# Seven block products for eight in the gate and value products of three FFN units (sparse attention and gated FFN, one core)

## The chip, the cores and the metric

The kernel runs on one core of one Trainium2 chip. The metric is the device time of one execution in microseconds. The core's engines are TensorE (PE), VectorE (DVE), ScalarE (ACT), GpSimd (POOL) and SyncE (SP, which only issues DMAs here). Each engine works through its own queue in order; semaphores tie them together. The program is written with a fixed order: nothing decides at run time which step comes next.

## The reference, cut to what matters

```
# 1. attention: q, k, v are [4, 8, 768, 64]; chunks of 32 keys, each query may use its 6 best chunks
ub     = sum(max(q * k_min(chunk), q * k_max(chunk)))      # bound of a chunk, causal
scores = q @ k.T / 8, masked to the 6 chunks with the largest ub and to earlier keys
attn   = softmax(scores) @ v
# 2. FFN: x is [3072, 512], the 8 heads side by side
gate = 1 / (1 + exp(-(x @ w_gate)))        # w_gate [512, 1536]
val  = x @ w_val                           # w_val  [512, 1536]
out  = (gate * val) @ w_out                # w_out  [1536, 512]
```

## The kernel before, in words

The 24 blocks of 128 queries (four batches of six) are worked in eight units, u0 to u7; units 1 to 7 have up to three blocks, 384 tokens. For each unit the kernel prepares keys and queries, chooses chunks, runs attention (`attend`, L880: scores on TensorE, exponentials on ScalarE, causal mask on GpSimd, attention times values on TensorE) and leaves the transposed result `xT` in SBUF, four tiles of 128 input features by 384 tokens in f16. Then `ffn` (L1062) makes the FFN of the unit.

In `ffn` the 1536 hidden features are 12 column blocks (`fb`) of 128. For each, TensorE makes the gate product `g` (four matmuls of 384 columns, L1078) and the value product `v` (four more) into a PSUM bank each. ScalarE takes tanh of half the gate (L1087), and VectorE makes `hg = (tanh + 1) * v` from SBUF and PSUM (L1091); the missing factor 0.5 is applied at the output. `hg` is f16.

The output product has two forms. Units 0 to 3 use plain matmuls (L1119) and a copy out of PSUM (L1128). Units 4 to 7 use `pair` (L989): two token blocks of 128, two halves of every group of four hidden blocks and two halves of the output columns make a 2 x 2 by 2 x 2 block product, which is computed with seven block products (p1 to p7, L1013) for eight, in Winograd's form. It needs sums of blocks beforehand (`sw` and `sx`, L1000, on VectorE or GpSimd; of the output weights `tw`, L984, made once) and additions afterwards (L1030, VectorE, from PSUM). The third token blocks of two neighbouring units are held (`held`, L409 and L411 by engine) and paired with each other (u45, u67).

The order of everything is written out: the string `ORDER` (L96) names each step with its engine in the order in which it is emitted, and `SLOTS` (L250) fixes which slot of a rotating buffer each tile takes (PSUM has eight slots, `ps`, of a bank each). `plan.add` names a step with the engines that it may use and its dependencies; `Plan.order` (L77) reads the two strings. The costs that stand beside the steps do not reach the program.

Of the kernel before, what the change touches and what calls it, by code (L numbers as in the profile page):

```python
# [8 lines left out]
F32 = mybir.dt.float32  # L9
# [99 lines left out]
hq0=V mx0_u1=V ap0_u1=V apt0_u1=V hqm0_u1_0=G v_u0_0=P v_u0_2=P v_u0_3=P hg_u0_3=V wo0=G hkp111=G ubn1_u1=V tanh_u0_0=A hq0_u1_1=A
tanh_u0_1=A hg_u0_0=V v_u0_1=P hg_u0_1=V hg_u0_2=V v_u0_7=P v_u0_4=P hqm0_u1_2=A sc_u1_0_2=P exp_u1_0_2=A sc_u1_2_2=P sc_u1_2_0=P  # L110
sc_u1_0_1=P sc_u1_2_1=P exp_u1_0_1=A v_u0_5=P g_u0_5=P tanh_u0_5=A hq1_u1_0=V kcr1=V hk0_u1_3=V hg_u0_5=V g_u0_7=P tanh_u0_7=A
wo1=G hk0_u1_1=G hq1_u1_2=G hkf1=G hk1_u1_0=G hq1_u1_3=G exp_u1_2_1=A g_u0_4=P tanh_u0_4=A hg_u0_7=V ubm1_u1=V mx1_u1=V ap1_u1=V
apt1_u1=V sc_u1_3_2=P exp_u1_3_2=A exp_u1_2_2=A exp_u1_2_0=A cm_u1_2=G sc_u1_1_0=P sc_u1_1_2=P sc_u1_3_1=P exp_u1_1_2=A v_u0_6=P
sc_u1_0_0=P sc_u1_3_0=P g_u0_6=P exp_u1_3_1=A exp_u1_1_0=A tanh_u0_6=A exp_u1_3_0=A hg_u0_4=V hg_u0_6=V sc_u1_1_1=P v_u0_9=P
v_u0_8=P v_u0_10=P g_u0_10=P tanh_u0_10=A exp_u1_1_1=A hg_u0_10=V g_u0_9=P tanh_u0_9=A g_u0_11=P tanh_u0_11=A exp_u1_0_0=A
g_u0_8=P tanh_u0_8=A v_0_3=S wo2=G cm_u1_3=G hqm1_u1_2=G v_0_1=S v16_0_1=G v_0_2=S v16_0_3=G v16_0_2=G pv_u1_3=P pv_u1_2=P
hqm1_u1_0=G sc_u1_4_2=P exp_u1_4_2=A sc_u1_4_1=P sc_u1_5_1=P exp_u1_5_1=A exp_u1_4_1=A sc_u1_5_2=P o0_u0_0=P rz_u1_1=V x_u1_1=V
hg_u0_9=V xps_u1_1=P xT_u1_1=V exp_u1_5_2=A sc_u1_4_0=P exp_u1_4_0=A cm_u1_0=G pv_u1_0=P cm_u1_1=G pv_u1_1=P rz_u1_0=V hg_u0_8=V
x_u1_0=V sc_u1_6_0=P exp_u1_6_0=A sc_u1_6_2=P exp_u1_6_2=A sc_u1_7_0=P v_u0_11=P sc_u1_6_1=P q2_u2=S k0_u2=S kn_u2_0=A qn_u2_2=G
qT_u2_2=P exp_u1_6_1=A sc_u1_7_2=P exp_u1_7_2=A qf_u2_2=V hq0_u2_2=A sc_u1_7_1=P xps_u1_0=P sc_u1_5_0=P xT_u1_0=A exp_u1_5_0=A  # L120
exp_u1_7_1=A kT_u2_0=P kx1_u2_0=V o0_u0_1=P exp_u1_7_0=A qf1_3=S cm_u1_6=G pv_u1_6=P o1_u0_0=P hg_u0_11=V kt_u2_0=V o2_u0_0=P
kx0_u2_0=V q0_u2=S k2_u2=S kn_u2_2=A kT_u2_2=P kx0_u2_2=V kx1_u2_2=V kt_u2_2=V cm_u1_5=G qn_u2_0=G qT_u2_0=P cm_u1_7=G pv_u1_7=P
rz_u1_3=V osb_u0_0=A pv_u1_5=P q3_u2=S qn_u2_3=G cm_u1_4=G qT_u2_3=P k1_u2=S kn_u2_1=A kT_u2_1=P kx0_u2_1=V pv_u1_4=P k3_u2=S
kn_u2_3=G kT_u2_3=P hk0_u2_0=G hq1_u2_2=G qf_u2_0=A hq1_u2_0=G q1_u2=S qn_u2_1=A qT_u2_1=P o1_u0_1=P kf1_3=S kf0_3=S kfT_3=P
kt_u2_1=A qf_u2_1=A hk1_u2_1=A rz_u1_2=V x_u1_3=V x_u1_2=V xps_u1_2=P xps_u1_3=P qf0_3=S qfT_3=P o2_u0_1=P kx1_u2_3=V kx0_u2_3=V
vf1_3=G qm_u2_1=G qm_u2_0=G hk1_u2_0=A qm_u2_2=A qf_u2_3=A qm_u2_3=A xT_u1_3=V kx1_u2_1=V kcr_u2=G ub_u2=P xT_u1_2=A hk0_u2_2=A
kf16_3=V qf16_3=A scf_3=P vf_3=S vc_3=A out_u0_0=S expf_3_1=A expf_3_0=A hq0_u2_3=A hk0_u2_1=G hq0_u2_0=G kt_u2_3=A g_u1_0=P
g_u1_1=P tanh_u1_0=A o0_u0_2=P osb_u0_1=V hq0_u2_1=V hq1_u2_1=A tanh_u1_1=A cmf_3_0=G pvf_3_0=P o1_u0_2=P o2_u0_2=P osb_u0_2=A
ubn0_u2=V ubn1_u2=V mx1_u2=V mx0_u2=V ap1_u2=V rzf_3_0=V apt1_u2=V cmf_3_1=G hqm1_u2_0=G sc_u2_5_2=P xf_3_0=V pvf_3_1=P
sc_u2_4_0=P exp_u2_4_0=A xpsf_3_0=P sc_u2_4_1=P exp_u2_5_2=A exp_u2_4_1=A sc_u2_5_1=P sc_u2_5_0=P exp_u2_5_0=A ap0_u2=V apt0_u2=V  # L130
hqm0_u2_0=V sc_u2_0_1=P exp_u2_0_1=A sc_u2_0_0=P xTf_3_0=V rzf_3_1=V sc_u2_1_0=P sc_u2_1_2=P xf_3_1=V v_u1_0=P hg_u1_0=V
sc_u2_0_2=P g_u1_2=P v_0_4=S hqm1_u2_2=G hqm0_u2_2=G v_0_5=S v16_0_5=G hq1_u2_3=G v16_0_4=G exp_u2_0_0=A cm_u2_0=G cm_u2_5=G
# [226 lines left out]
def kernel(  # L359
# [17 lines left out]
    T = 384  # L377
# [684 lines left out]
    def ffn(u, base, span):  # L1062
# [4 lines left out]
        for fb in range(NFB):  # L1067
# [17 lines left out]
            if fb % 2 == 0:  # L1085
                plan.hold(op, hg)
# [171 lines left out]
```

## Time and profile before

| What | Value |
|---|---|
| Runs of the kernel before | 289.1, 288.9 and 289.47 us, median 289.1 |
| The profiled execution's own time | 288.62 us |
| Its span, first to last instruction | 286.6 us |
| Output product of unit 4 begins | 199.84 us |
| Last TensorE instruction ends | 282.8 us |

The profile shows one execution. A busy time is the time in which at least one instruction of that engine was under way. A group of instructions has its line, engine, operation and tiles (`out<-in`), the count, the busy time, the mean length of one in ns, and the idle time of its engine just before them with what ended it. A row of the timeline has start, length, engine and line, and the number of merged instructions (`x3`). A row of waits has the engine that waited, the one that released it, the total in us, the number of waits and the longest. Line numbers are those of the kernel before.

### The profile page before, as it was taken

How to read it: one execution, taken by the hardware profiler on the slowest of the kernel's cores; microseconds unless marked ns; L12 is line 12 of the kernel's file. 1: busy time of each engine (PE TensorE's matmuls, PEld its weight loads, DVE VectorE, ACT ScalarE, POOL GpSimd, SP SyncE). 2: the span in 40 equal slices, each digit the busy share in tenths (PEclk: the TensorE clock that was granted, in tenths of full speed). 3: DMA queues.
4: the chain of work that ended last, by engine and by line, in shares of the span. 5: the costliest groups of instructions: out<-in, count | busy, mean ns of one | idle time of the engine just before them, and what ended most of it. 6: DMA issues, size and time to landing. Idle time of an engine off the chain costs nothing.

```text
span 286.6 us, 7277 instructions
## 1 busy us (share of the span) xinstructions
PE 272.8 (95%) x2764; PEld 186.3 (65%) x2764; DVE 212.3 (74%) x615; ACT 186.9 (65%) x392; POOL 148.2 (52%) x233
## 2 busy tenths in 40 slices
PE   3878999999999999999999999999999999999994
PEld 2654566667755765556677548767876786676673
DVE  3678846687999989796989997866725756373785
ACT  5688578779976965369999769997763402514210
POOL 6567773768394803926677765655611080130430
PEclk9999999999999999999999999999999999999999
DMA  7999999999999994799950030000020020000124
GB/s 166 238 221 195 196 204 223 249 174 204 175 206 188 163 193 104 160 162 243 173 113 2 0 113 2 2 0 2 2 77 0 1 75 0 2 0 0 68 81 183
DMA packets 123377, 32.69 MB, mean 114 GB/s; under 512 B 111440, under 2 KB 120400, under 8 KB 123344
## 3 DMA queue, kind: packets, MB, share of 16 engines
q1 hardware_dynamic: 118592, 27.53, 45.9%
q0 software_dynamic: 4752, 4.72, 9.8%
q8 instruction: 21, 0.34, 0.5%
q14 instruction: 12, 0.10, 0.1%
HBM read 30.67 MB, written 6.29 MB: 129 GB/s over the span
## 4 chain that ended last, share of the span: by engine, by line
PE 81%; DMA 12%; SPq 2%; POOL 1%; DVE 1%; issue 1%; DVEq 0%
PE g_u L1078 19%; PE v_u L1078 19%; PE sc_u L896 11%; PE o_u L1119 10%; PE p_u L1013 9%; PE pv_u L929 6%; DMA wo<-in_moe_w_out_dram 5%; DMA wg<-in_moe_w_gate_dram 4%; PE ube_u L835 2%; DMA kq_u<-in_q_dram 2%; PE xps_u L956 1%; SPq L586 1%; DMA kf<-in_k_dram 1%; SPq L575 1%; DVE ox L1030 1%
## 5 line engine op out<-in xcount | busy, mean ns | idle before, releaser
L907 ACT ACTIVATE att_u<-sc_u 128x512 f16<-128x512 f32 (+3 forms) x184 | 86.8, 570 | 5.0 <-PE sc_u L896 2.5
L1087 ACT ACTIVATE gate_u<-g_u 128x384 f16<-128x384 f32 x96 | 47.1, 503 | 58.4 <-PE g_u L1078 53.1
L1091 DVE SCALAR_TENSOR_TENSOR hg_u<-gate_u,v_u 128x384 f16<-128x384 f16 x96 | 50.8, 543 | 36.0 <-PE v_u L1078 20.9
L1078 PE MATMUL g_u<-xT_u,wg 128*128 128x384 f16 x384 | 73.2, 326 | 0.9 <-DMA wg<-in_moe_w_gate_dram 0.9
L1078 PE MATMUL v_u<-xT_u,wv 128*128 128x384 f16 x384 | 72.5, 326 | 0.0
L1078 PEld LDWEIGHTS <-wg 128*128 128x128 f16 x384 | 36.0, 98 | 24.5 <-DMA wg<-in_moe_w_gate_dram 1.8
L1078 PEld LDWEIGHTS <-wv 128*128 128x128 f16 x384 | 36.2, 98 | 22.9 <-issue 0.5
L913 POOL TENSOR_SCALAR_AFFINE_SELECT att_u<-att_u 128x384 f16<-128x384 f16 (+1 forms) x56 | 28.2, 514 | 36.1 <-ACT att_u L907 30.6
L1119 PE MATMUL o_u<-wo,hg_u 128*128 128x512 f16 x144 | 34.6, 379 | 0.4 <-DMA wo<-in_moe_w_out_dram 0.3
L929 PE MATMUL pv_u<-v,att_u 128*128 128x65 f16 x640 | 26.6, 193 | 0.0
L929 PEld LDWEIGHTS <-att_u 128*128 128x128 f16 x640 | 24.5, 98 | 2.2
L896 PE MATMUL sc_u<-hqo,hko 128*128 128x128 f16 (+2 forms) x220 | 25.7, 243 | 0.0
L896 PE MATMUL sc_u<-hqe,hke 128*128 128x128 f16 (+2 forms) x220 | 25.1, 243 | 0.0
L1119 PEld LDWEIGHTS <-hg_u 128*128 128x128 f16 x144 | 13.5, 98 | 13.9 <-issue 0.6
L612 POOL CAST v<-v 128x512 f16<-128x512 f32 x23 | 13.7, 613 | 15.0 <-DMA v<-in_v_dram 14.7
L896 PEld LDWEIGHTS <-hke 128*128 128x128 f16 x220 | 16.7, 98 | 5.3 <-ACT xT_u L407 0.6
L896 PEld LDWEIGHTS <-hko 128*128 128x128 f16 x220 | 16.2, 98 | 4.3 <-DVE hqo L409 0.2
L636 POOL TENSOR_SCALAR qm_u<-qf_u 128x768 f32<-128x768 f32 (+3 forms) x10 | 16.2, 1617 | 3.3 <-PE ubo_u L835 2.0
L1030 DVE SCALAR_TENSOR_TENSOR sw<-p_u,sw 128x256 f32<-128x256 f32 (+1 forms) x20 | 10.6, 529 | 6.1 <-PE p_u L1013 5.7
L948 DVE TENSOR_TENSOR x_u<-pv_u,rz_u 128x384 f16<-128x384 f32 (+1 forms) x28 | 14.5, 525 | 0.4
L858 DVE MAX8 mx_u<-ubn_u 128x8 f32<-128x8 f32 (+16 forms) x152 | 12.6, 159 | 0.3
L1128 ACT ACTIVATE osb_u<-o_u 128x512 f32<-128x512 f32 x10 | 6.0, 596 | 10.1 <-PE o_u L1119 10.1
(159 smaller groups left out, 442.5 us busy)
## 6 DMA issues: line engine op xcount, KB each, us to landing
v<-in_v_dram SPq DMA_DIRECT2D x23, 256.0 KB, 4.4
k<-in_k_dram SPq DMA_DIRECT2D x12, 384.0 KB, 5.5
q<-in_q_dram SPq DMA_DIRECT2D x12, 384.0 KB, 5.5
out_dram<-osb_u SPq DMA_DIRECT2D x12, 256.0 KB, 3.4
out_dram<-sw SPq DMA_DIRECT2D x8, 256.0 KB, 2.0
wg<-in_moe_w_gate_dram POOLq DMA_DIRECT2D x3, 512.0 KB, 11.5
wv<-in_moe_w_val_dram POOLq DMA_DIRECT2D x3, 512.0 KB, 11.2
wo<-in_moe_w_out_dram POOLq DMA_DIRECT2D x3, 512.0 KB, 13.2
```

The lines of the kernel that those rows point to most:

```text
L612: plan.add(f"v16_{b}_{ib}", {POOL: pool(H * D)}, lambda e: nc.gpsimd.tensor_copy(v16[b % 2][:, ib, :, 0:D], at(t)), reads=[t], writes=[("v ...
L636: (nc.vector if e == DVE else nc.gpsimd).tensor_scalar_max(o, i, 0.0)
L896: nc.tensor.matmul(at(t)[:, o:o + 128 * m], hk[b % 2][e_][:, p, 128 * jb:128 * jb + 128], hq[u.side][e_][:, p, 128 * x:128 * (x + m)], sta ...
L907: plan.add(f"exp_{u.name}_{h}_{y}", {ACT: act(n)}, lambda e, t=t, att=att, b0=b0, n=n: nc.scalar.activation(at(att)[:, b0:b0 + n], at(t), ...
L913: nc.gpsimd.affine_select(out=dv, in_=dv, compare_op=ALU.is_ge, fill=0.0, base=0, pattern=[[0, u.m], [1, 128]], channel_multiplier=-1)
L929: nc.tensor.matmul(at(pv)[:, last, x, :], at(att)[:, c:c + 128], v16[b % 2][:, jb, h, :], start=(jb == 0), stop=(jb == ib))
L948: plan.add(f"x_{u.name}_{p}", {DVE: dve(u.t)}, lambda e: nc.vector.tensor_tensor(at(x_).rearrange("p a (e d) -> p e a d", e=2), at(pv)[:, ...
L1013: nc.tensor.matmul(at(to)[:, side], a(j)[:, i], b(j)[:, i], start=j == i == 0, stop=j == 2 and i == 1)
L1078: nc.tensor.matmul(at(t), w16[:, c, 128 * fb:128 * fb + 128], at(u.xt)[:, c, :], start=(c == 0), stop=(c == 3))
L1087: plan.add(f"tanh_{u.name}_{fb}", {ACT: act(T)}, lambda e, g=g, gate=gate: nc.scalar.activation(at(gate), at(g), AF.Tanh, scale=0.5), read ...
L1091: plan.add(f"hg_{u.name}_{fb}", {DVE: dve(T)}, lambda e, w_=w_, gate=gate, hg=hg, fb=fb: nc.vector.scalar_tensor_tensor(at(hg)[:, fb % 2], ...
L1119: nc.tensor.matmul(at(o), at(hgs[fc // 2])[:, fc % 2, 128 * tb:128 * tb + 128], wo16[:, fc, lo:hi], start=(fc == 0), stop=(fc == NFB - 1))
```

## The change

In units 5, 6 and 7 part of the gate and value products also goes by seven block products. Two neighbouring column blocks of 128 hidden features, two halves of the 512 input features and two halves of 192 tokens make the 2 x 2 by 2 x 2 product. `BY7` says which: column pairs 1 to 4 (blocks 2 to 9) of units 5 and 6, pairs 1 and 2 (blocks 2 to 5) of unit 7, gate and value each; 20 products of pairs. The other column blocks keep the plain products.

- For a pair there are seven products of two matmuls of 192 columns (`by7`), in four PSUM banks (p1; p2 and p6; p5 and p3; p7 and p4), where there were eight matmuls of 384 columns in two banks.
- The weights' sums (`ss`, four f16 sums of 256 elements for each of the eight weight pairs, 32 in all) are made once, those of x (`tt`, four f16 sums of 384 for each unit, 12 in all) for each unit.
- After the products, a copy `m1` takes p1 out of PSUM, and six additions per pair make the four blocks in f32 in SBUF (`c11` of 384 elements; `c4`, `c3`, `c12`, `c22`, `c21` of 192). For value pairs all six are on VectorE and read PSUM. For gate pairs (`SLOW7`) three copies on ScalarE (`m26`, `m53`, `m74`, 384 elements each) first bring the products into SBUF as f32, and the additions are spread over VectorE (25) and GpSimd (35).
- tanh and `hg` of these column blocks read the f32 result from SBUF and not from PSUM.
- Space: the copies lie in the first key buffer (`hk[0]`), free once unit 6's scores are made; the weights' sums in the buffers of raw v and in `v16[0]`; the sums of x in `hk[0]` or in the unit's query buffer.
- `ffn(units[5])` is planned behind the attention of unit 6 and no longer ahead of it. `ORDER` and `SLOTS` are new throughout the kernel: 1826 steps became 2140 (40 removed, 354 added: TensorE 140, VectorE 124, ScalarE 48 and GpSimd 42 of the added), and 162 of the steps that both have changed their engine.

```
+    SLOW7 = {(u, "g", i) for u in (5, 6, 7) for i in (1, 2, 3, 4)}
+    BY7 = {u: {(m, i) for i in (1, 2, 3, 4)[:2 if u == 7 else 4] for m in "gv"} for u in (5, 6, 7)}
...
+    def sums_of(u, next_):
...
+                w, out_ = blocks_of(m, i), ss[m, i]
+                for n, (a, b, op) in enumerate(((lambda w=w: w(1, 0), lambda w=w: w(1, 1), ALU.add), (out_[0][1], lambda w=w: w(0, 0), ALU.subtract),
+                                                (lambda w=w: w(0, 0), lambda w=w: w(1, 0), ALU.subtract), (lambda w=w: w(0, 1), out_[1][1], ALU.subtract))):
+                    plan.add(f"ss{n}_{m}{i}", {DVE: dve(256, 2), POOL: pool2(256)}, lambda e, a=a, b=b, op=op, o=out_[n][1]: both(e).tensor_tensor(
+                        o(), a(), b(), op), ...
...
+        for n, (a, b) in enumerate(((lambda: x_(0, 1), lambda: x_(0, 0)), (lambda: x_(1, 1), lambda: t_(0)),
+                                    (lambda: x_(1, 1), lambda: x_(0, 1)), (lambda: x_(1, 0), lambda: t_(1)))):
+            plan.add(f"tt{n}_{u.name}", {DVE: dve(384, 2), POOL: pool2(384)}, lambda e, a=a, b=b, n=n: both(e).tensor_tensor(
+                t_(n), a(), b(), ALU.subtract), ...
...
+    def by7(u, m, i, next_, views):
...
+        def product(p, to, side, a, b, reads):
+            def emit(e):
+                for c in range(2):
+                    nc.tensor.matmul(at(to)[:, side], a()[:, c], b()[:, c], start=c == 0, stop=c == 1)
...
+        p1, p26, p53, p74 = bank("p1", 1), bank("p26"), bank("p53"), bank("p74")
+        op = product("p1", p1, 0, lambda: w(0, 0), lambda: x_(0, 0), [])
+        product("p2", p26, 0, lambda: w(0, 1), lambda: x_(1, 0), [])
+        product("p6", p26, 1, s7[1][1], lambda: t_(1), tk(1))
+        product("p5", p53, 0, s7[0][1], lambda: t_(0), tk(0))
+        product("p3", p53, 1, s7[3][1], lambda: x_(1, 1), [s7[3][0]])
+        product("p7", p74, 0, s7[2][1], lambda: t_(2), tk(2))
+        product("p4", p74, 1, lambda: w(1, 1), lambda: t_(3), [(f"tt{u.i}", 3)])
...
+        move("m1", p1, lambda: v_(2), 1, [p1], [q[2]])
+        if slow:
+            tmp = Buf("tm", f"tm_{name}", [128, 3, 2, 192])
+            move("m26", p26, lambda: at(tmp)[:, 0], 2, [p26, ("tt5", 0)], [(tmp, 0)])
+            move("m53", p53, lambda: at(tmp)[:, 1], 2, [p53], [(tmp, 1)])
+            move("m74", p74, lambda: at(tmp)[:, 2], 2, [p74], [(tmp, 2)])
...
+        def onto(p, n, src, dst, other, reads, writes):
+            plan.add(f"{p}_{name}", {POOL: pool2(192 * n), DVE: dve(192 * n)} if slow else {DVE: dve(192 * n)}, lambda e: both(e).tensor_tensor(
+                dst(), src[0](), other(), ALU.add), ...
+        onto("c11", 2, a26, lambda: v_(0, 2), lambda: v_(2).to_broadcast([128, 2, 192]), [q[2]], [q[0], q[1]])
+        onto("c4", 1, a5, lambda: v_(3), lambda: v_(1), [q[1]], [q[3]])
+        onto("c3", 1, a7, lambda: v_(2), lambda: v_(1), [q[1]], [q[2]])
+        onto("c12", 1, a3, lambda: v_(1), lambda: v_(3), [q[3]], [q[1]])
+        onto("c22", 1, a7, lambda: v_(3), lambda: v_(3), [q[3]], [q[3]])
+        onto("c21", 1, a4, lambda: v_(2), lambda: v_(2), [q[2]], [q[2]])
...
     def ffn(u, base, span):
...
+                if seven[0]:
+                    gs = by7(u, "g", fb // 2, next_, views)
+                if seven[1]:
+                    vs = by7(u, "v", fb // 2, next_, views)
...
-    ffn(units[5], 6.0, 0.95)
...
     attend(units[6], 6.0)
+    ffn(units[5], 6.0, 0.95)
```

More of the change, by code (lines that the diff above doesn't have):

```diff
@@ L331 @@
+p7_u67:5 p4_u67:1
 """
@@ L397, in at @@
     def at(b):
+        if b.tile is None and b.kind == "tm":
+            b.tile = hk[0][b.slot].rearrange("p a s -> p (a s)")[:, 0:2304].bitcast(F32).rearrange("p (n x r) -> p n x r", n=3, x=2)
         if b.tile is None:
@@ L1060, in store @@
             dma=((hi - lo) * 1.35, 2048 if hi - lo > 256 else 512))
+    SLOW7 = {(u, "g", i) for u in (5, 6, 7) for i in (1, 2, 3, 4)}
+    BY7 = {u: {(m, i) for i in (1, 2, 3, 4)[:2 if u == 7 else 4] for m in "gv"} for u in (5, 6, 7)}
+    combos = sorted(set().union(*BY7.values()), key=lambda w: (w[1], "vg".index(w[0])))
+    old = [("v16", 0, ib) for ib in range(NBLK)]
+    keys0 = [("hk", 0, jb, e_, p) for jb in range(NBLK) for e_ in range(2) for p in range(NP)]
+    ss = {}
+    for n, w in enumerate(combos):
+        if n < 6:
+            b = Buf("v", f"ss_{w[0]}{w[1]}", [128, 4, 2, 128], F16)
+            ss[w] = [((b, x), lambda b=b, x=x: at(b)[:, x]) for x in range(4)]
+        else:
+            ss[w] = [(("ss", n, x), lambda n=n, x=x: v16[0].rearrange("p a h d -> p (a h d)")[
+                :, 1024 * (n - 6) + 256 * x:1024 * (n - 6) + 256 * x + 256].rearrange("p (i f) -> p i f", i=2)) for x in range(4)]
@@ L1067, in ffn @@
         for fb in range(NFB):
-            g = ps(f"g_{u.name}_{fb}", "ff", [128, T])
-            w_ = ps(f"v_{u.name}_{fb}", "ff", [128, T])
-            gate = Buf("gate", f"gate_{u.name}_{fb}", [128, T], F16)
+            seven = [u.i in BY7 and (m, fb // 2) in BY7[u.i] for m in "gv"]
             if fb % 2 == 0:
                 hgs.append(Buf("hg", f"hg_{u.name}_{fb // 2}", [128, 2, T], F16))
+                if seven[0]:
+                    gs = by7(u, "g", fb // 2, next_, views)
+                if seven[1]:
+                    vs = by7(u, "v", fb // 2, next_, views)
             hg = hgs[-1]
+            gate = Buf("gate", f"gate_{u.name}_{fb}", [128, T], F16)
             def product(t, w16, fb=fb):
```

573 lines of the change are left out of this document (331 added, 242 removed), and 2 rows, old and new, of the table plan.

## The prediction

> **What bounds the kernel now.** I read the page first, then TensorE's waits, then the windows.
>
> ```profile
> span 286.6 us, 7277 instructions
> PE 272.8 (95%) x2764; PEld 186.3 (65%) x2764; DVE 212.3 (74%) x615; ACT 186.9 (65%) x392; POOL 148.2 (52%) x233
> PE   3878999999999999999999999999999999999994
> PEclk9999999999999999999999999999999999999999
> PE 81%; DMA 12%; SPq 2%; POOL 1%; DVE 1%; issue 1%; DVEq 0%
> ```
>
> TensorE (PE) is busy for 95% of the span at full clock, and it is 81% of the chain that ended last. So a product less is worth its full length, as long as TensorE still gets its operands and its PSUM banks in time. Next, the windows: from 40 us to the first output product of unit 4, from there to TensorE's last product, the tail, and one earlier stretch for comparison.
>
> ```profile
> 40.00:199.84 159.84, 159.40 (x1817) 106.67 (x1816) 132.71 (x403) 128.85 (x275) 97.87 (x149) 1.00 0.69 132
> 199.84:282.80 82.96, 82.26 (x711) 59.44 (x709) 50.60 (x126) 29.98 (x66) 23.57 (x38) 1.00 0.10 36
> 282.80:286.60 3.80, 0.01 (x1) 0.00 (x0) 0.82 (x2) 0.00 (x0) 0.00 (x0) 1.00 0.39 138
> 80.00:100.00 20.00, 20.00 (x193) 12.00 (x192) 19.16 (x56) 16.27 (x37) 14.83 (x22) 1.00 1.00 185
> ```
>
> The columns are PE, PE's weight loads, DVE, ACT and POOL. All of the seven-product work lies in the second row. There TensorE idles 0.70 us in 82.96, VectorE (DVE) is busy 50.60, ScalarE (ACT) 29.98 and GpSimd (POOL) 23.57. TensorE's only wait there is this one:
>
> ```profile
> PE p_u L1013 <- DVE held L409: 0.7, 1, 0.7
> ```
>
> So that stretch has free time on three engines and none on TensorE. The question is whether 82.96 us has room for what the change puts on those three.
>
> **What it removes: 2.84 us of TensorE.** Three pieces of the chain in order of time (start, length, instructions) and one group:
>
> ```profile
> 206.49 0.91 PE pv_u L929 x30
> 217.56 1.95 PE v_u L1078 x12
> 230.84 6.11 PE p_u L1013 x56
> L929 PEld LDWEIGHTS <-att_u 128*128 128x128 f16 x640 | 24.5, 98 | 2.2
> ```
>
> One matmul costs 0.91/30 = 30.3 ns at 65 columns, 6.11/56 = 109.1 ns at 256 and 1.95/12 = 162.5 ns at 384. The line between the first two gives 82.7 ns at 192. A pair of column blocks takes 8 x 162.5 = 1300 ns now and 14 x 82.7 = 1158 ns then: 142 ns less, 20 times, is 2.84 us. A weight load lasts 98 ns, more than 82.7, but the 65-column matmuls come every 30.3 ns with one load each, so loads overlap and I charge nothing. Without that overlap a pair takes 14 x 98 = 1372 ns, 72 more than now.
>
> The Trainium skill's "TensorE: Matmul & The Clock Gate", section "Back-to-back issue gap", speaks against the change: it gives a sustained 81 ns per matmul at 128 columns and 131 at 512. On its line 192 columns would cost 89 ns and 384 columns 114 ns, so a pair would grow from 915 to 1251 ns, an estimate of 6.7 us lost in all. The rows (30.3 at 65, 162.5 at 384) lie on neither of its figures, so the trace decides and the sum doesn't use it.
>
> **What it adds to VectorE: about 30 us in the same stretch.** The lengths come from these rows:
>
> ```profile
> 226.85 0.55 DVE L948 TENSOR_TENSOR x_u<-pv_u,rz_u 128x384 f16<-128x384 f32 x1
> 227.31 0.18 DVE L946 RECIPROCAL rz_u<-pv_u 128x6 f32<-128x6 f32 x1
> 228.51 0.28 DVE L1000 TENSOR_TENSOR sw<-hg_u,hg_u 128x256 f16<-128x256 f16 x1
> 228.72 0.28 DVE L1000 TENSOR_TENSOR sx<-held,hg_u 128x256 f16<-128x256 f16 x1
> L1030 DVE SCALAR_TENSOR_TENSOR sw<-p_u,sw 128x512 f32<-128x512 f32 x8 | 5.5, 688 | 3.2 <-PE p_u L1013 3.1
> L1030 DVE SCALAR_TENSOR_TENSOR sw<-p_u,sw 128x256 f32<-128x256 f32 x12 | 5.1, 423 | 2.9 <-PE p_u L1013 2.5
> ```
>
> Back to back, the next instruction starts 0.09 us before the last one ends: 0.46 us from start to start at 384 elements, 0.21 for an f16 sum of 256. An addition from PSUM grows by (688 - 423)/256 = 1.04 ns an element, so 192 elements last 0.36 us and cost 0.27. The order that the new kernel fixes puts these on VectorE after unit 4's first output product (in both kernels TensorE has about 190 us of work, by these spacings, queued ahead of it):
> - value pairs, all on VectorE: 10 x (one of 384, five of 192) = 10 x 1.81 = 18.1 us;
> - gate pairs, VectorE's part: 4 of 384 and 21 of 192 = 7.5 us, and 2 moves, 0.5;
> - 15 of the 32 weight sums at 0.21 and 11 of the 12 sums of x at 0.27: 6.2 us. The other weight sums stand earlier, beside full TensorE work; I charge nothing for them.
>
> That is 32.3 us. Against it, 8 sums, 4 copies and 2 scalings move to the other engines, and a few steps of unit 7's attention move in: about -2.3. VectorE goes from 50.60 to 80.6 us where TensorE needs 82.96 - 2.84 = 80.1. The 50.60 counts instructions that stood alone at full length; if all but a third of those 126 overlap by 0.08 us, it falls by 6 to 7, to 74. I take the middle, 77.
>
> **What it adds to the others.**
>
> ```profile
> L984 POOL TENSOR_TENSOR tw<-wo,tw 128x512 f16<-128x512 f16 x2 | 2.3, 1152 | 0.0
> L1000 POOL TENSOR_TENSOR sw<-sw,hg_u 128x256 f16<-128x256 f16 x4 | 2.7, 670 | 9.7 <-DVE sw L1000 9.6
> L1087 ACT ACTIVATE gate_u<-g_u 128x384 f16<-128x384 f32 x36 | 16.9, 491 | 41.4 <-PE g_u L1078 38.4 <-DVE hg_u L1091 3.0
> ```
>
> GpSimd grows by (1152 - 670)/256 = 1.88 ns an element: 0.55 us at 192 and 0.91 at 384. Six of 384 and 29 of 192 are 21.4 us; with 3 weight sums, one sum of x, 7 more sums for the output and 2 copies, some 30 us: 23.6 becomes 53. ScalarE gets 30 moves of 384 (0.49 each) and 18 shorter ones, about 20 us: 50 of 80. Neither is the bound by itself.
>
> **What VectorE and GpSimd do to each other.** No row has f32 sums on both engines at once. The nearest:
>
> ```profile
> 202.10 2.29 POOL L1000 TENSOR_TENSOR sw<-hg_u,sw 128x256 f16<-128x256 f16 x3 [0.83 <-DVE sw L1000]
> 202.21 0.84 DVE L984 TENSOR_TENSOR tw<-wo,tw 128x512 f16<-128x512 f16 x1
> 208.29 0.42 DVE L984 TENSOR_TENSOR tw<-wo,tw 128x512 f16<-128x512 f16 x1
> 121.27 2.29 POOL L612 CAST v<-v 128x512 f16<-128x512 f32 x4
> 122.94 0.92 DVE L863 TENSOR_TENSOR ap<-ubn_u,mx_u 128x288 f16<-128x288 f32 x1
> 126.62 0.46 DVE L863 TENSOR_TENSOR ap<-ubn_u,mx_u 128x288 f16<-128x288 f32 x1
> L984 DVE TENSOR_TENSOR tw<-wo,tw 128x512 f16<-128x512 f16 x4 | 2.0, 522 | 0.0
> L1000 DVE TENSOR_TENSOR sx<-hg_u,hg_u 128x256 f16<-128x256 f16 x4 | 1.6, 409 | 0.0
> L1000 DVE TENSOR_TENSOR sx<-sx,held 128x256 f16<-128x256 f16 x3 | 1.2, 403 | 1.0 <-POOL sx L1000 1.0
> ```
>
> A VectorE sum with both inputs in SBUF takes twice its time when GpSimd is in an instruction: 0.84 for 0.42, 0.92 for 0.46, in f16 and from f32. The means show what that costs over the stretch: the last three groups lose (522 - 420) x 4, (409 - 280) x 4 and (403 - 280) x 3 ns, 1.3 us over 11 instructions. The other 28 output sums there run close to 0.28, so I spread 1.3 to 2.2 us over some 39: up to 0.056 each, while GpSimd was busy 28% of the time. In the new kernel GpSimd is busy 53 of 80 us, 66%, and about 105 VectorE instructions have both inputs in SBUF: 30 output sums, 15 weight sums, 11 sums of x, 4 of the output weights, 25 gate additions, and 20 gate-times-value steps whose value now lies in SBUF and not in PSUM (that last kind is not shown by any row). The upper end is 105 x 0.056 x 66/28 = 14 us; the lower end is nothing, if the order keeps them apart. I take 5, nearer the lower end, because most of today's sums meet nothing.
>
> The Trainium skill says in "SBUF — State Buffer", section "Who interferes with whom", that a VectorE instruction with two SBUF inputs and a GpSimd instruction that reads SBUF exclude each other for their whole length. The pairs 0.84/0.42 and 0.92/0.46 agree; what it makes of the sum is a rival below.
>
> **The sum.** VectorE: 77 + 5 = 82 us. It can't be fed without a gap: in the densest earlier window it was busy 19.16 of 20, so 82 takes 82 x 20/19.16 = 85.6 us, against 82.96 now: +2.6. Each value pair holds four of the eight PSUM banks until VectorE's last addition, and TensorE's queue is in order, so a late addition stops the next pair's first product and the plain products and output products behind it. What precedes the stretch I leave as it is. The order there is new as well; these are TensorE's longest waits before 40 us behind the first load:
>
> ```profile
> PE qT_u L734 <- POOL qn_u L411: 1.0, 1, 1.0
> PE pvf L699 <- POOL attf L692: 1.0, 2, 0.7
> ```
>
> One of them more or less is 0.5 to 1 us either way, which I put at nothing. The tail of 3.80 us stays: the same sums and stores end it. The profiled execution took 288.62 us; 288.62 + 2.6 = 291.2. The median of the runs shown, 289.1, is 0.5 above it: 291.7 us.
>
> **The rivals.**
> - *Faster, TensorE stays the bound (35%).* If VectorE's work and waits come to less than 80.1 us, the end moves by the removed products: -2.84, 286.3 on the median; with one or two stalls 287. For it: 74 is my lower end, and today's order keeps TensorE at 82.26 of 82.96. Against it: 77 us before any wait on GpSimd leaves 3. Break-even is 82.96 of VectorE time; within 0.2% of it I put 7%.
> - *The two engines exclude each other fully (11%).* GpSimd's 53 us and the 30 us of two-input VectorE work (30 x 0.21 + 15 x 0.21 + 11 x 0.27 + 4 x 0.36 + 7.5 + 20 x 0.46) can't overlap at all: 83 us packed without a gap, and much of it stands in the seven-product stretches of units 5 and 6. With the upper 14 us of waits VectorE needs 77 + 14 = 91, over 0.958 is 95: +12, 301 on the median; halfway, 296. For it: the two doubled rows. Against it: most f16 sums today run at 0.28. By the page on SBUF this is what must happen.
> - *The products aren't cheaper (4%).* If 98 ns a weight load sets the pace, a pair costs 72 ns more: 20 x 0.072 = +1.4, 290.5. Against it: 30.3 ns at 65 columns.
>
> **How the numbers follow.** The forecast, VectorE as the bound with modest waits, has 43%; with 11 and 4 that makes 58% slower, 7% the same and 35% faster (0.2%, 0.6 us, is about what a measurement of this kernel can tell from no change). The likeliest case by itself runs from 289.8 to 295. The range must reach the TensorE-bound end, 286.3, since that case holds a third, and part of the exclusive case: 286.3 to 297.5, leaving out the full 14 us of waits and a gain larger than the removed products.
>
> **What would show it.** In the new trace: matmuls of 192 columns at 82 to 84 ns (98 would be the third rival); VectorE busy over 90% from unit 4's output products on; TensorE waits on the additions and moves of the seven products, 4 to 6 us in sum (under 1 us is the first rival); two-input VectorE groups with means well over their shortest, the sums of x, weight sums and gate additions first; gate-times-value steps of seven-product blocks longer than 549 ns. I am wrong if VectorE stays under 85% there and TensorE is still busy over 98%, or if TensorE waits for GpSimd or ScalarE instead.

## The result and the profile after

| | before | after |
|---|---|---|
| Median of the runs beside each other | 289.29 us (288.9 to 289.92) | 297.06 us (296.58 to 298.71) |
| Ratio, 95% interval | | 1.0277 [1.0232, 1.0321] |
| Profiled execution, span | 288.62, 286.6 us | 296.58, 294.9 us |
| Unit 4's first output product to TensorE's last | 82.96 us | 91.30 us |

The change makes the kernel 2.8% slower, about 7.8 us. (Here and below the ratio is an estimate of its own over the undisturbed runs and can differ a little from the ratio of the medians; runs of different sessions are compared by their ratios.) The page of after, the lines that answer to those of before:

```profile
span 294.9 us, 7765 instructions
PE 271.7 (92%) x2884; PEld 192.3 (65%) x2884; DVE 253.0 (86%) x724; ACT 209.5 (71%) x452; POOL 182.0 (62%) x278
PE   3769979999999999999999999999989799899993
PEclk9899999999999999999999999999999999999998
PE 60%; DVE 20%; DMA 10%; issue 3%; ACT 3%; SPq 2%; POOL 1%; DVEq 0%; ACTq 0%; POOLq 0%
```

TensorE's share of the chain that ended last fell from 81% to 60% and VectorE's rose from 1% to 20%. In the row of slices TensorE is full from the seventh slice to the 29th; from the 30th on (about 214 us) it has gaps, at full clock (1.00 in the window of the stretch below). The windows of after (PE, weight loads, DVE, ACT, POOL) say where:

```profile
40.00:199.80 159.80, 158.80 (x1820) 106.49 (x1820) 139.18 (x425) 127.91 (x273) 94.39 (x144) 1.00 0.67 129
199.80:291.10 91.30, 83.62 (x830) 66.59 (x826) 88.25 (x219) 50.47 (x122) 59.02 (x85) 1.00 0.10 37
291.10:294.90 3.80, 0.00 (x0) 0.00 (x0) 0.32 (x1) 0.00 (x0) 0.00 (x0) 0.65 0.37 126
220.00:240.00 20.00, 16.62 (x174) 13.37 (x174) 19.41 (x44) 9.42 (x22) 13.01 (x19) 1.00 0.00 1
```

Unit 4's output product begins at 199.80 (199.84 before) and the tail is 3.80 us as before, so the whole loss of these two executions, 8.3 us of span, lies between. There VectorE is busy 88.25 of 91.30 us. In the 20 us in which TensorE does worst (16.62 busy) VectorE is busy 19.41. The page's waits of TensorE in that stretch, the longest ones:

```profile
PE p_u L1054 <- DVE hg_u L1252: 1.4, 1, 1.4
PE p_v_u L1163 <- DVE hg_u L1252: 0.7, 1, 0.7
PE p_v_u L1163 <- DVE f_v_u L1200: 0.7, 1, 0.7
PE p_g_u L1163 <- DVE f_v_u L1200: 0.7, 2, 0.5
PE p_u L1054 <- DVE sw L1041: 0.7, 1, 0.7
```

Nearly all are on VectorE. The listed waits come to 6.3 us, but they are not all: a busy time counts a matmul that stands alone at its full length in the trace (246 ns at 192 columns), not at its spacing (82.5 ns). Counted from the start of one matmul to the start of the next, against the undisturbed spacing (82.5 ns at 192 columns, 109.1 at 256, 162.5 at 384, and so on the same line), the 824 matmuls from unit 4's first output product to the last one hold 79.19 us of work in 90.10 us, so 10.9 us of **stalls**. Before it was 81.88 in 82.86, 1.0 of stalls. Work -2.7, stalls +9.9. I use this count for every run below.

What VectorE's time went to is seen in its groups in this stretch (mean ns behind the busy time):

```profile
L1252 DVE SCALAR_TENSOR_TENSOR hg_u<-gate_u,f_v_u 128x384 f16<-128x384 f16 x20 | 14.9, 758 | 0.3
L1252 DVE SCALAR_TENSOR_TENSOR hg_u<-gate_u,v_u 128x384 f16<-128x384 f16 x21 | 10.9, 543 | 0.8 <-ACT gate_u L1243 0.7
L1200 DVE TENSOR_TENSOR f_g_u<-hke,f_g_u 128x192 f32<-128x192 f32 x14 | 8.4, 600 | 0.3
L1200 DVE TENSOR_TENSOR f_v_u<-p_v_u,f_v_u 128x192 f32<-128x192 f32 x50 | 16.2, 348 | 0.5
L1143 DVE TENSOR_TENSOR hqe<-xT_u 128x384 f16<-128x384 f16 x4 | 1.8, 456 | 0.0
L1130 DVE TENSOR_TENSOR ss_g<-wg,ss_g 128x256 f16<-128x256 f16 x3 | 0.8, 282 | 0.0
```

The same step takes 758 ns with both inputs in SBUF (`gate`, `f_v`) and 543 with one in PSUM; the same addition 600 and 348. How that comes about is seen in the timeline:

```profile
230.83 2.71 DVE L1200 TENSOR_TENSOR f_g_u<-hko,f_g_u 128x192 f32<-128x192 f32 x4
231.06 0.78 POOL L1041 TENSOR_TENSOR sw<-hg_u,hg_u 128x256 f16<-128x256 f16 x1
231.81 0.78 POOL L1041 TENSOR_TENSOR sx<-hg_u,hg_u 128x256 f16<-128x256 f16 x1
232.55 0.78 POOL L1041 TENSOR_TENSOR sx<-held,hg_u 128x256 f16<-128x256 f16 x1
233.29 0.78 POOL L1041 TENSOR_TENSOR sw<-sw,hg_u 128x256 f16<-128x256 f16 x1
233.46 1.00 DVE L1252 SCALAR_TENSOR_TENSOR hg_u<-gate_u,v_u 128x384 f16<-128x384 f16 x2
234.06 0.60 PE L1054 MATMUL p_u<-wo,hg_u 128*128 128x256 f16 x4 [1.44 <-DVE hg_u L1252]
```

Four gate additions on VectorE, 0.35 us each by themselves, take 2.71 us, one to each GpSimd sum of 0.78 (0.67 by itself). Behind them stands the `hg` step on which TensorE waits 1.44 us. From the first addition to the last of these sums it is 3.24 us (230.83 to 234.07); four of each by themselves add up to 4 x 0.35 + 4 x 0.67 = 4.1, or to 3.6 counted from start to start (0.27 and 0.63), so at this place the two exclude each other for most of their time, not for all of it.

### The profile page after: what moved, and what is told of

Its sections match the earlier page's. It is cut to its first block, busy times and chain, and to the rows that moved or that the text cites. A ratio compares the mean times of both kernels' runs of the same rounds, so it can differ in the third digit from the quotient of the medians.

```text
span 294.9 us, 7765 instructions
## 1 busy us (share of the span) xinstructions
PE 271.7 (92%) x2884; PEld 192.3 (65%) x2884; DVE 253.0 (86%) x724; ACT 209.5 (71%) x452; POOL 182.0 (62%) x278
## 4 chain that ended last, share of the span: by engine, by line
PE 60%; DVE 20%; DMA 10%; issue 3%; ACT 3%; SPq 2%; POOL 1%; DVEq 0%; ACTq 0%; POOLq 0%
PE v_u L1231 11%; PE g_u L1231 11%; PE o_u L1280 10%; PE sc_u L937 9%; DMA v<-in_v_dram 8%; PE pv_u L970 6%; PE p_u L1054 5%; DVE hg_u L1252 5%; DVE f_g_u L1200 4%; DVE f_v_u L1200 4%; PE ube_u L876 2%; SPq L616 2%; PE xps_u L997 1%; PE p_v_u L1163 1%; DVE sw L1041 1%
## 5 line engine op out<-in xcount | busy, mean ns | idle before, releaser
L1231 PE MATMUL g_u<-xT_u,wg 128*128 128x384 f16 x304 | 58.3, 326 | 2.6 <-DMA wg<-in_moe_w_gate_dram 2.4
L1231 PE MATMUL v_u<-xT_u,wv 128*128 128x384 f16 x304 | 57.6, 326 | 1.2 <-DVE hg_u L1252 0.7
L1243 ACT ACTIVATE gate_u<-g_u 128x384 f16<-128x384 f32 x76 | 37.1, 500 | 27.4 <-PE g_u L1231 24.2
L1252 DVE SCALAR_TENSOR_TENSOR hg_u<-gate_u,v_u 128x384 f16<-128x384 f16 x76 | 39.7, 541 | 13.6 <-ACT gate_u L1243 9.3
L1231 PEld LDWEIGHTS <-wg 128*128 128x128 f16 x304 | 28.3, 98 | 20.6 <-DMA wg<-in_moe_w_gate_dram 3.0
L1231 PEld LDWEIGHTS <-wv 128*128 128x128 f16 x304 | 28.7, 98 | 18.7 <-issue 2.5
L1200 DVE TENSOR_TENSOR f_v_u<-p_v_u,f_v_u 128x192 f32<-128x192 f32 (+1 forms) x60 | 21.4, 382 | 0.6
L1200 POOL TENSOR_TENSOR f_g_u<-hko,f_g_u 128x192 f32<-128x192 f32 (+1 forms) x22 | 16.4, 751 | 4.6 <-DVE f_g_u L1200 3.5
L1243 ACT ACTIVATE gate_u<-f_g_u 128x384 f16<-128x384 f32 x20 | 10.3, 522 | 11.0 <-DVE f_g_u L1200 5.7
L1252 DVE SCALAR_TENSOR_TENSOR hg_u<-gate_u,f_v_u 128x384 f16<-128x384 f16 x20 | 14.9, 758 | 0.3
```

The source lines that it names most:

```text
L1200: plan.add(f"{p}_{name}", {POOL: pool2(192 * n), DVE: dve(192 * n)} if slow else {DVE: dve(192 * n)}, lambda e: both(e).tensor_tensor(dst( ...
L1231: nc.tensor.matmul(at(t), w16[:, c, 128 * fb:128 * fb + 128], at(u.xt)[:, c, :], start=(c == 0), stop=(c == 3))
L1243: plan.add(f"tanh_{u.name}_{fb}", {ACT: act(T, not seven[0])}, lambda e, gv=gv, gate=gate: nc.scalar.activation(at(gate), gv(), AF.Tanh, s ...
L1252: plan.add(f"hg_{u.name}_{fb}", {DVE: dve(T)}, lambda e, vv=vv, gate=gate, hg=hg, fb=fb: nc.vector.scalar_tensor_tensor(at(hg)[:, fb % 2], ...
```

## The experiments

**Theory 1**: VectorE's steps with two SBUF inputs and GpSimd's sums hold each other up; this lengthening is the loss. (At first it was put as waits of VectorE alone; after the first four kernels it was restated as each side waiting for the other.) **Rival 2**: VectorE's added work alone fills it. **Rival 3**: the fixed order, its PSUM slots and its chains over three engines stall TensorE whatever the lengths are. The first seven kernels start from after; times are medians with the ratio to runs of before on the same chip (288.2 to 288.9 us). The first four ran together.

**pool_only_writes.**

```
-        return nc.vector if e == DVE else nc.gpsimd
+        return nc.vector if e == DVE else OnlyWrites   # memset(o) three times up to 256 elements, else twice
```

> The changed kernel, but each sum or addition of two tiles that its order gives to GpSimd (35 gate additions and the block sums) only writes its output, with two or three memsets in place of the addition; that arithmetic is left out, GpSimd stays busy for about as long, and every wait and order stays. Theory 1 (VectorE is the bound because about 13 of its 88 us in the stretch from unit 4's output products on are waits for GpSimd instructions that read SBUF at the same time): gate-times-value of the seven-product blocks falls from a mean of 758 ns to about 545, VectorE's gate additions of 192 elements from 600 to about 350, VectorE's busy time in the stretch from 88 to about 76 us, and the time to 286.5 to 289.5 us. Rival 2 (VectorE's own work is the bound, the waits are hidden): time stays at 294 to 297. Rival 3 (TensorE's stalls come from the order and the PSUM banks, not from VectorE's load): VectorE's busy time may fall, the time stays at 294 to 297.

Measured: 294.20 us, 1.0195 [1.0161, 1.0228]; stalls 7.0. The groups, the stretch with the 20 us that were worst in after, and two of GpSimd's rows at that place:

```profile
L1258 DVE SCALAR_TENSOR_TENSOR hg_u<-gate_u,f_v_u 128x384 f16<-128x384 f16 x20 | 10.9, 555 | 2.2 <-ACT gate_u L1249 2.0
L1206 DVE TENSOR_TENSOR f_g_u<-hke,f_g_u 128x192 f32<-128x192 f32 x14 | 4.9, 351 | 1.6 <-POOL f_g_u L1016 1.3
```

```profile
201.50:288.00 86.50, 83.20 (x830) 66.84 (x826) 76.87 (x218) 49.38 (x122) 65.15 (x226) 1.00 0.10 38
220.00:240.00 20.00, 18.23 (x187) 14.45 (x185) 16.19 (x48) 9.27 (x23) 17.76 (x63) 1.00 0.01 1
```

```profile
227.21 1.05 POOL L1016 MEMSET sw<- 128x256 f16 x3
228.19 0.89 POOL L1016 MEMSET f_g_u<- 128x192 f32 x3
```

The lengthening is gone (758 to 555, 600 to 351), and VectorE's busy time fell to 76.87 us, although GpSimd is busier than in after (65.15 us of the stretch for 59.02). So it is what GpSimd's sums read that does it. By the ratios only 0.8%, about 2.4 us, came back, though: theory 1's time failed, and 294.20 lies in the 294 to 297 of rivals 2 and 3. But three memsets take 1.05 us for a sum of 0.67 to 0.78, and GpSimd (17.76 of 20) had become the chain itself. The test was confounded; pool_two_writes mends it.

**value_adds_little.** The last four additions of a value pair cover 8 of 192 columns (c11, c4 whole).

> The changed kernel, but four of the six additions of each value pair (c3, c12, c22, c21; 40 instructions on VectorE that read PSUM and one SBUF tile, which no wait for GpSimd lengthens) cover 8 of their 192 columns; that arithmetic is left out. It takes 40 x 0.19 = 7.7 us from VectorE and leaves what GpSimd and VectorE do to each other. Theory 1 and rival 2 (VectorE is the bound, with or without the waits): the time falls by nearly all of it, to 289 to 291 us. Rival 3 (the order and the banks stall TensorE): 295 to 297.

Measured: 294.47 us, 1.0209 [1.0175, 1.0244]; stalls 8.25.

```profile
200.15:287.90 87.75, 82.33 (x831) 66.67 (x827) 81.03 (x217) 50.17 (x122) 60.47 (x85) 1.00 0.10 35
```

VectorE's busy time in the stretch falls from 88.25 to 81.03 us, and the time by 0.7%, about 2 us. That is 3.5 us above the number of theory 1 and rival 2 and 0.5 below that of rival 3, so by itself it speaks rather for rival 3. VectorE's load plays a part, but is not the whole. The steps with two SBUF inputs stay as long as in after (`hg` 766 ns).

**gate_only and value_only.** `BY7` is cut to the gates, then to the values; the others get plain products again, put into the order of after at the first place with a free PSUM slot.

> The change undone for the ten value pairs: they are plain products again, the ten gate pairs stay by seven; the order of the rest is that of the changed kernel. TensorE gets back 10 x 0.142 = 1.4 us of work; VectorE loses 18 us of value additions, 1.6 of sums and the 4.3 us by which gate-times-value had grown (its value is read from PSUM again), so it needs about 64 us where TensorE needs 81.5. Theory 1 and rival 2: TensorE is the bound again, 287.5 to 289.5 us; the gate additions on VectorE keep most of their length (about 500 to 600 ns) by theory 1, about 350 by rival 2. Rival 3: 292 to 297, since the order is the same.

> The change undone for the ten gate pairs: they are plain products again, the ten value pairs stay by seven; the order of the rest is that of the changed kernel. VectorE loses 7.5 us of gate additions and their 6 us of waits, GpSimd 20 us, ScalarE 15 us. VectorE then needs about 71 us where TensorE needs 81.5. Theory 1: 287.5 to 289.5 us, and gate-times-value of the seven-product blocks drops to 600 to 650 ns because GpSimd is busy less. Rival 2: VectorE's 80 us without the gate part would leave it just under TensorE, 288 to 290, with gate-times-value unchanged near 758 ns. Rival 3: 292 to 297.

Measured: 306.63 us, 1.0634 [1.0594, 1.0674], and 312.58 us, 1.0833 [1.0775, 1.0891]; stalls 19.3 and 24.8. TensorE's longest wait in each:

```profile
PE v_u L1214 <- DVE hg_u L1235: 5.7, 3, 4.4
```

```profile
PE g_u L1210 <- DVE f_v_u L1179: 6.6, 5, 2.4
```

Half the pairs, and slower than all, above every number that was expected: the plain products wait for slots that are given back late. So these two show what a badly placed product costs (rival 3 is real as a mechanism), and their times show nothing of pairs. The lengths bear out theory 1 as far as they go: the gate additions take 481 and 529 ns in gate_only (350 by themselves), and `hg` falls to 568 in value_only, where no gate addition is left on GpSimd.

**pool_two_writes.** The confound removed: two memsets everywhere.

> GpSimd's sums and additions are replaced by two memsets of the same output (arithmetic left out); three of them, as pool_only_writes had, took 0.77 us at 192 f32 and 1.05 at 256 f16 in its timeline, longer than the sums they stood for (0.55 and 0.67 where nothing disturbs), so GpSimd itself had become the chain. Two take about 0.57, 0.65 and 0.78 (192, 256, 384), at or just under the sums' undisturbed time. Theory 1, restated (the exclusion of two-input VectorE work and GpSimd sums, in which each side waits for the other, makes the stalls; the order is sound without it): the stalls fall from 10.9 us to 1 to 2, the stretch from 90.1 to about 81, the time to 287 to 288.5. Rival (the in-order queues and chains stall whatever the exclusion does): VectorE's two-input steps are as short as in pool_only_writes, yet 5 to 7 us of stalls stay, 292 to 294.

Measured: 286.84 us, 0.9947 [0.9923, 0.9970]; stalls 0.86. The stretch, and the group:

```profile
201.29:281.62 80.33, 80.31 (x830) 66.90 (x826) 76.58 (x218) 49.98 (x122) 46.37 (x159) 1.00 0.11 41
```

```profile
L1258 DVE SCALAR_TENSOR_TENSOR hg_u<-gate_u,f_v_u 128x384 f16<-128x384 f16 x20 | 10.8, 552 | 0.4 <-ACT gate_u L1249 0.2
L1206 DVE TENSOR_TENSOR f_g_u<-hke,f_g_u 128x192 f32<-128x192 f32 x14 | 4.9, 349 | 0.2
```

Whether GpSimd is kept as long as by its sums is seen in its rows, two of this kernel and two sums of after that meet no step of VectorE with two SBUF inputs:

```profile
223.71 0.57 POOL L1016 MEMSET f_g_u<- 128x192 f32 x2 [1.18 <-ACT f_g_u L448]
227.08 0.68 POOL L1016 MEMSET sw<- 128x256 f16 x2
```

```profile
271.40 0.59 POOL L1200 TENSOR_TENSOR f_g_u<-hke,f_g_u 128x192 f32<-128x192 f32 x1
269.47 0.67 POOL L1041 TENSOR_TENSOR sw<-hg_u 128x256 f16<-128x256 f16 x1
```

Theory 1, restated, holds, a little under its numbers: same order, same waits, VectorE's work whole, GpSimd kept nearly as long as by sums that nothing disturbs (at 384 elements, seven sums, 0.89 us for 1.00), and TensorE is busy 80.31 of 80.33 us. Rival 3 falls as the cause of after's stalls, and so does rival 2, since VectorE's 76.58 us of work fit. The order has little to spare, though: with GpSimd's third memset, pool_only_writes, 6 us of stalls come back. With the sums' reading taken out, and nearly the same time on GpSimd, the kernel is 0.5% faster than before.

**all_adds_little.** One memset for each of GpSimd's sums, and all additions of VectorE but c11 and c4 at 8 columns.

> GpSimd's sums and additions are one memset each, and of VectorE's additions of the seven products all but the first two of a pair (c11, c4) cover 8 of 192 columns (arithmetic left out); every instruction, wait and bank hand-over stays in its place. This is the order with both the exclusion and most of the added work taken out. Theory 1 restated: nothing left to wait for, stalls under 1.5 us, stretch 80 to 81, time 286.3 to 287.8, hardly below pool_two_writes. Rival 2 (VectorE's load by itself): 286.3 to 287.8 too, but clearly below pool_two_writes (by 2 us or more). Rival 3 (order, banks, chains): 290 or more.

Measured: 286.22 us, 0.9938 [0.9917, 0.9959]; stalls 0.14.

```profile
199.98:279.60 79.62, 79.59 (x829) 67.18 (x825) 67.91 (x218) 49.62 (x122) 25.10 (x85) 1.00 0.11 41
```

VectorE loses another 8.7 us of work (67.91 busy), GpSimd 21 (25.10 busy), and the time moves by 0.6 us, inside the intervals: rival 2 falls as a sole cause here too. VectorE's 76.6 us fit into the stretch; 88 don't.

**pool_one_read.** A memset and a copy of the first input for each of GpSimd's sums.

> As pool_two_writes, but the second memset is a copy of the sum's first input to the output, so that GpSimd reads SBUF once for some 0.4 us per sum and writes for some 0.3 (arithmetic left out). It asks what in GpSimd's work excludes VectorE's two-input steps. If reading as such does it: gate-times-value steps of seven-product blocks between 555 and 758 ns on the mean, some 650, stalls of 3 to 6 us, 289 to 292.5. If only GpSimd instructions with two inputs do it: as pool_two_writes, 555 ns and 286.5 to 287.5.

Measured: 290.13 us, 1.0061 [1.0031, 1.0092]; stalls 4.1.

```profile
L1258 DVE SCALAR_TENSOR_TENSOR hg_u<-gate_u,f_v_u 128x384 f16<-128x384 f16 x20 | 11.7, 593 | 0.7 <-ACT gate_u L1249 0.5
L1206 DVE TENSOR_TENSOR f_g_u<-hke,f_g_u 128x192 f32<-128x192 f32 x14 | 5.4, 389 | 0.5 <-POOL f_g_u L1016 0.2
```

With GpSimd reading one input for 0.4 us per sum, the time is 3.3 us above pool_two_writes and VectorE is busy 79.77 us for 76.58; the step's mean (593) rose less than I had put (650). So a GpSimd instruction with one input holds VectorE up as well. How much of the 3.3 us that makes is not shown: a memset and a copy also last longer than two memsets, 0.66 us for 0.57 at 192 elements and 0.77 for 0.68 at 256.

The next kernels change the amount. Behind unit 4's attention their order, engines and slots are made anew so that, by lengths close to the traces', GpSimd's steps stand away from VectorE's steps with two SBUF inputs.

**eight_pairs and six_values.**

```
+    BY7 = {5: {g1, g2, v1, v2}, 6: the same, 7: {}}     # eight_pairs, from the order of before
+    BY7 = {5: {v1, v2, v3}, 6: the same, 7: {}}         # six_values, from the order of before
```

> Eight of the twenty pairs by seven products (gate and value of column blocks 1 and 2 in units 5 and 6), the rest plain; order and buffers of the kernel before up to 40 steps ahead of unit 4's output products, and behind that an order made anew in which GpSimd's sums stand away from VectorE's two-input steps. TensorE's work falls by 8 x 0.142 = 1.14 us against before, VectorE gets 8 x 1.8 us of additions at most, some 65 of 81 us. Theory 1 restated (the exclusion, in sum with VectorE's load, is the price; where there is room for both the products are worth their full length): 0.7 to 1.2 us under before, ratio 0.996 to 0.998, stalls under 1 us. Rival (seven products cost TensorE stalls by their chains and banks whatever the room): the same or 1 to 3 us slower than before.

> Six value pairs alone by seven products (column blocks 1 to 3 in units 5 and 6), none of the gates; order behind the same place made anew in the same way. No addition of the seven products is on GpSimd, none has both inputs in SBUF. TensorE's work falls by 6 x 0.142 = 0.85 us, VectorE gets 6 x 1.81 = 10.9 us and 12 sums. Theory 1 restated: 0.5 to 0.9 us under before, ratio 0.997 to 0.998, against 312.6 for value_only, whose plain gates stood badly: so that its time came from the order it was put in, not from value pairs. Rival: as slow as before or slower.

Measured: eight_pairs 287.80 us, 0.9979 [0.9951, 1.0007], stalls 1.6; six_values 286.59 us, **0.9944 [0.9920, 0.9969]**, stalls 0.1. The second beats both kernels, by more than the 0.2 to 0.3% expected. Its window:

```profile
200.00:281.25 81.25, 81.24 (x742) 61.64 (x738) 68.57 (x173) 32.93 (x72) 29.78 (x45) 1.00 0.09 34
```

TensorE has no gap left, with VectorE at 68.57 of 81.25 and GpSimd at 29.78. The rival (stalls whatever the room) falls; for eight pairs the interval reaches no change, and the stalls of 1.6 us are more than the 1 us expected.

**no_pairs and six_gates**, made in the same way: no pair at all, and `BY7 = {5: {g1, g2, g3}, 6: the same}`.

> The control of six_values: no pair by seven products, the same products as before, and the order behind unit 4's attention made anew in the same way. If six_values owes its 1.6 us to the fewer products (0.85 us of TensorE's work by the spacings) and to the 0.98 us of TensorE stalls that the old order had, this one shows the second alone: 0 to 0.9 us under before, ratio 0.997 to 1.000, and 0.7 to 1.2 above six_values. If the new order is the whole of it: 0.994 like six_values.

> Six gate pairs (column blocks 1 to 3 in units 5 and 6) by seven products and no value pair, order made anew in the same way; about half of the pairs' additions stand on GpSimd, the other half on VectorE with both inputs in SBUF, so this has the kind of work that excludes. If the exclusion costs only where VectorE has no room left (theory 1 restated): TensorE's work falls by 0.85 us and the time is that of six_values within 0.8 us, ratio 0.993 to 0.998. If gate pairs cost by their kind whatever the room is: 1 to 3 us slower than six_values.

Measured: no_pairs 288.96 us, 1.0003 [0.9969, 1.0037]; six_gates 287.64 us, 0.9929 [0.9900, 0.9959], both with stalls under 0.4. So the new order alone gives nothing that can be measured, and six_values gains by its pairs: the distance of the two ratios, 0.6%, is more than the 0.85 us (0.3%) of the products, but the intervals hold 0.3% as well. Gate pairs are as good as value pairs where there is room, with 17 of their 36 additions on GpSimd and most of VectorE's lengthened only to 431 and 435 ns. The stretch of six_gates:

```profile
200.00:283.97 83.97, 83.88 (x786) 63.94 (x783) 69.29 (x154) 39.21 (x88) 53.80 (x82) 1.00 0.09 33
```

GpSimd is busy 53.80 us and VectorE 69.29 of 83.97, so lengthened steps cost TensorE next to nothing here, where VectorE has time left.

**twenty_again.** All twenty pairs, order behind unit 4's attention made anew from that of after.

> The whole change, all twenty pairs, with order, engines and buffers behind unit 4's attention made anew so that GpSimd's sums stand away from VectorE's two-input steps where that can be (31 of 60 gate additions on GpSimd for 35, eight fewer sums on it in all). If the price is mostly the order's, which was made without regard to the exclusion: 287 to 289. If it is mostly the amount (VectorE's two-input work and GpSimd's sums together nearly fill the stretch, so they can't be kept apart): a part comes back, 290 to 293. If neither: 296 as before.

Measured: 294.72 us, 1.0175 [1.0133, 1.0216]; stalls 6.6.

```profile
201.10:287.84 86.74, 82.93 (x844) 68.00 (x842) 82.43 (x229) 50.03 (x117) 48.36 (x71) 1.00 0.08 28
```

```profile
L1253 DVE SCALAR_TENSOR_TENSOR hg_u<-gate_u,f_v_u 128x384 f16<-128x384 f16 x20 | 11.5, 593 | 0.2
L1201 DVE TENSOR_TENSOR f_g_u<-hke,f_g_u 128x192 f32<-128x192 f32 x17 | 6.4, 398 | 0.1
```

About 1% came back, less than either case expected. The steps are mostly apart now (593 and 398 for 758 and 600), but sums that GpSimd gave up stand on VectorE, which is busy 82.43 of 86.74. This one order avoids neither. Whether another would, and which of the 6.6 us of stalls are VectorE's load and which the new order's own waits, stays open.

## Why the prediction was right or wrong

The sign was right and the range held, by 0.4 us at its upper end; the size was not: +7.8 us for the +2.6 forecast, and 297.06 is 5.4 us above the 291.7 and above the 289.8 to 295 of the likeliest case. The term that failed is the waits of VectorE on GpSimd.

- *TensorE, -2.84 us: right.* By spacing the stretch lost 2.69 us of work. A row of the chain in order of time of after: eight matmuls of 192 columns in 0.66 us, 82.5 ns each.

```profile
245.35 0.66 PE p_v_u L1163 x8
```

The third rival (98 ns) is refuted. So is the line through the figures of the Trainium skill's "TensorE: Matmul & The Clock Gate", section "Back-to-back issue gap", which I had shown beside the sum and not used.

- *VectorE, 77 us without waits: right.* pool_two_writes has 76.58, with nothing held up. The 77 was the middle of 74 and 80.6, so that it fits to 0.4 us is partly luck.
- *GpSimd 53 us, ScalarE 50: right as sizes.* GpSimd was busy 59.02 with its own waits (a sum that met nothing took 0.59 us at 192 elements and 1.00 at 384, for 0.55 and 0.91), ScalarE 50.47.
- *Waits on GpSimd, 5 us of 0 to 14: the step that failed.* The trace of after has 88.25 - 76.58 = 11.7 us, 0.11 us for each of the 105 steps. By groups against pool_two_writes: `hg` 20 x 0.21 = 4.1, gate additions 21 x 0.245 = 5.1, output sums and sums of x 2.5. My reason for the lower half, that most of today's sums meet nothing, did not carry over: what I scaled by GpSimd's busy share came out at 0.13 us an instruction, and the steps that I had not seen in any row (the `hg` steps) or that come in runs of four beside runs of four (the timeline above) lost 0.21 to 0.25. My upper end, 14, was close. Before, 8 of VectorE's 41 output sums in the whole kernel overlapped a GpSimd sum; in the new order 17 of the 20 `hg` steps and 18 of the 21 gate additions of 192 elements do.
- *Feeding: right.* VectorE was busy 96.7% of the stretch (88.25/91.30), where I took 95.8%. 11.7 us in place of 5 is 7.0 us of time at 95.8%; 76.58 for 77 takes back 0.4 and the better feeding 0.8. That is the miss: a stretch of 91.30 us where the sum had 85.6.
- *Head and tail unchanged: right for after* (199.80 and 3.80). In pool_two_writes, where TensorE is the bound, the profiled execution reaches the stretch at 201.29 us, 1.45 later than before, and the tail is 286.1 - 281.62 = 4.5 us; of the 2.6 us gained in the stretch 0.5 are left. Why the stretch begins later there was not looked into.
- *The rivals.* The first had a condition that failed. Its price was right for the stretch: in pool_two_writes it is 2.6 us shorter than before. For the whole kernel it was too high: 286.84 lies in its 286.3 to 287, but beside runs of before with a median of 288.35 that is 1.5 us gained, where it had 2.1 to 2.8. The second named the cause; its halfway value 296 was nearer than my forecast. Its full exclusion is not what the timeline shows (3.24 us for 3.6 at the least). The Trainium skill's "SBUF — State Buffer", section "Who interferes with whom", says that a VectorE instruction with two SBUF inputs contends with a GpSimd instruction that reads SBUF and not with one that only writes. The runs agree: 758 ns beside sums, 593 beside copies, 555 beside memsets.
- *Signs.* VectorE over 90%, TensorE's waits on additions and moves, and long gate additions, sums of x (456 for 341) and `hg` steps came as named. The weight sums did not lengthen (282). The waits, 6.3 on the page, are 10.9 by spacing.

## What to carry to other kernels

Work that leaves TensorE must be priced with what it does to its neighbours: where VectorE is to be nearly filled (it was busy 97% of the stretch in after, 95% in twenty_again, and 83% in six_gates, which lost 0.3 us in stalls), sums with two SBUF inputs on VectorE and sums on GpSimd are not to be laid beside each other. Adding them up as if on one engine is the careful count; in the timeline above it would be 3.6 us or more for the 3.24 measured. Do as many pairs as fit: six of twenty, 6 x 0.142 us of TensorE's work, gained, eight showed no clear change, and twenty lost 2.8%. An experiment that takes a cause away must keep the other engine's durations, or it tests something else.

## What the runs showed of the hardware

A VectorE copy from SBUF to SBUF in f16, with one input, is held up as well. In eight_pairs:

```profile
257.32 0.71 POOL L1018 TENSOR_TENSOR sw<-hg_u,hg_u 128x256 f16<-128x256 f16 x1 [2.66 <-DVE hg_u L1230]
257.42 0.69 DVE L427 COPY held<-hg_u 128x256 f16<-128x256 f16 x1
```

Such a copy took 215 ns in six_values where it met no GpSimd step (at 208.38 us). An addition with one input in PSUM was not lengthened: the 50 of 192 elements took 348 ns on the mean and at most 358 in after, though 46 of them stood beside a GpSimd step, and 352 on the mean in pool_two_writes.
